# Attention chain in halves of heads, weight products in column halves, and new orders in a recurrent memory attention with its gradients

## The chip, the cores and the metric

The kernel runs on one core of one Trainium2 chip. The metric is the device time of one execution in microseconds (us); a kernel's time is the median of its runs. The core has five engines that work side by side: TensorE (PE in the profile, with its weight loads as PEld), VectorE (DVE), ScalarE (ACT), GpSimd (POOL) and SyncE (SP), which here only issues transfers (DMA). TensorE writes to PSUM, eight banks of 2 KB in each of 128 partitions. VectorE and ScalarE take results out of PSUM.

## The reference

The inputs are x (2048 tokens of 512), a memory of 8 rows, the weights of an attention with 32 heads of 128, those of an MLP with 1792 hidden units, and a gradient of the output. The attention goes over 64 segments of 32 tokens, one after the other, because the first 8 output rows of one segment are the memory of the next:

```python
for s in range(n_seg):                       # 64 segments of 32 tokens
    h = concatenate([mem, xn[:, 32 * s:32 * (s + 1)]])      # 8 + 32 rows
    q, k, v = (einsum('btd,dhe->bhte', h, W) for W in (Wq, Wk, Wv))
    p = softmax(where(mask, q @ k.T * Dh ** -0.5, -1e9))    # 40 x 40 a head
    o = einsum('bhte,hed->btd', p @ v, Wo)
    mem = o[:, :8]; outs.append(o[:, 8:])
out = x + concatenate(outs) + (relu(xn @ w1 + b1) ** 2 @ w2 + b2)   # xn = layernorm(x)
```

The outputs are out and its gradients with respect to x, the first memory, Wq, Wk, Wv, Wo, w1, b1, w2 and b2 for the given output gradient. The backward pass is again a recurrence, over the segments in reverse: the gradient that reaches a segment's memory rows is part of the output gradient of the segment before.

## The kernel before, in words

Five stages follow each other: layernorm and MLP (lines 640 to 910); the forward chain of 64 segments (stage built from line 920, `chain` at L1085); the turning of weights by TensorE transposes (`turn`, L449; `turn_o`, L464; called at L1231, L1232 and L1537); the backward chain (`chain`, L1454); and the weight gradients and layernorm gradient (from L1563).

**What sets the order.** Every piece of work is handed to a planner (`_Plan`, L74) with a cost for each engine that could do it, the keys that it reads and writes, and a priority (0 for the chain of the recurrence, 1 for the rest). The planner's `run` (L152) walks through time with these costs, gives each piece to an engine and writes the instructions of every engine in that order. The order is then fixed: an engine works through its own list and waits at its head. Two lists of numbers, `_FWD` (L27) and `_BWD`, raise or lower the rank of each kind of piece, and `_FWD_RULE`, `_BWD_RULE` and the two `_BIAS` pairs set its other rules.

**Layout.** A segment has 32 tokens and 32 heads. Heads lie as 4 (index j, a quarter of the partitions) by 8 (index i, along the columns). Most matmuls of the chain use TensorE as four column tiles of 128x32, so four matmuls with different j stand beside each other; the profile writes them `128*32`. Data of the two halves i = 0 to 3 and 4 to 7 have separate keys in several places.

**One forward segment** (`chain`, L1085) takes the rows in `hA` (named PA in the profile; one buffer holds a block of four segments) and does, in order: projections to q and k (`proj`, L493, matmuls at L501, two output halves of 512 columns, each 16 matmuls), evictions, transposes (`to_T`, L509, matmuls in L387), evictions; a mask matmul and the scores (L1101, L1109) into one bank of 128x320; the projection to v; then on DVE the maximum (L967), the subtraction (L968), on ACT the exponential (L971), on DVE a copy of the memory columns (L1114), two transposes (L1116, L1117), the sum (L1119) and reciprocal (L1120). `bd_fill` (L601, instructions at L603) writes the probabilities into block-diagonal tiles BDA and BDB, 4 copies of 32x256 each, on any of three engines. `bd` (L580, matmuls L588) multiplies them with v in two halves, DVE scales each half (L593) and transposes it (`sq_T`, L480, instruction L484) into OT. The output projection `wo_part` (L980, matmuls L988) runs 64 matmuls of 256 columns into one bank; ACT or DVE copies the bank to RFA (128x256); 16 small matmuls (L1138) select the memory rows, and one DVE copy (L1142) puts them into `hA` of the next segment. PSUM is dealt as four banks "c" for the chain in a ring, two "f" and two "m" for other work.

**Beside the forward chain** run the attention of the memory rows of whole blocks (`l_qkv`, L1025; `l_attn`, L1041), the block outputs (L1158) and the MLP's weight products (`dw_unit`, L1178, matmuls L1193), which accumulate 448 matmuls of 512 columns in two "m" banks from inputs `sx` loaded by SP.

**One backward segment** (`chain`, L1454) projects the output gradient, forms the gradients of the probabilities, goes back through the softmax, forms the three gradients dN of v, q and k (t = 2, 1, 0; `part_bd`, L1476), transposes each to dT, and sums their products with the weights into one bank "r" (`dh_part`, L1300, matmuls L1307, 64 of 512 columns for each t). Two copies of 256 columns bring the sum to R_A, 32 small matmuls (L1506) select the memory rows, and one DVE copy (L1510) puts them into `gT` for the next segment. SP issues loads and stores, among them the stores of dN (S_GN). Beside it run `l_pre` (L1318) and `l_post` (L1354).

## Time and profile before

| | us |
|---|---|
| runs before the change (3) | 2888.3, 2895.45, 2908.77 |
| median | 2895.45 |
| span of the profiled execution | 2892.0 |
| MLP stage | 0 to 226 |
| forward chain | 228 to 1230 |
| weight turns | 1230 to 1292 |
| backward chain | 1292 to 2306 |
| weight products | 2306 to 2892 |

The profile describes one execution; its own time is the span, 2892.0 us, measured from the first to the last instruction. The page gives the busy time of each engine. A group row has the line, the engine, the operation, what it writes and reads, the shape and the count, then total busy us and mean ns of one, then the idle time of the engine just before and what ended it. A row of the timeline has the start, the length, and what it merges (x16 is sixteen instructions); in square brackets stands the engine's wait before it and the instruction that ended that wait. A row of stages has the stretch, its length, the busy time of PE, PEld, DVE, ACT and POOL with their counts, the granted TensorE clock, the share of the transfer engines and GB/s.

### The profile page before, as it was taken

To read this page: it belongs to the slowest core of one execution; us is meant where nothing else is said; L and a number is where in the kernel's file an instruction comes from. 1 tells how busy PE (TensorE), PEld (TensorE's weight loads), DVE (VectorE), ACT (ScalarE), POOL (GpSimd) and SP (SyncE) were. 2 spreads that over 40 slices of the span, in tenths; PEclk is the share of its full clock that TensorE was granted. 3 is DMA by queue.
4 is the path that set the end of the run, shared out by engine and by line. 5 is a ranking of instruction groups with operands and counts; after the bars stand their busy time and mean duration, and the time that the engine had idled before them with its cause. 6 is when DMAs were issued, how large, how long until landed. Compare 5 with 4: busy or idle time off the path is not lost.

```text
span 2892.0 us, 110768 instructions
## 1 busy us (share of the span) xinstructions
PE 2679.4 (93%) x47273; PEld 1569.0 (54%) x47384; DVE 1366.9 (47%) x3432; ACT 1182.2 (41%) x2442; POOL 779.8 (27%) x1876
## 2 busy tenths in 40 slices
PE   8999999999889999888999989989999899999999
PEld 6665555555555555565555555555555544444444
DVE  5544555554554555574545545445454502232322
ACT  4334444454444554445555555555555510000000
POOL 1102221221221221234444434344343401111111
PEclk9999999999999999999999999999999999999999
DMA  6658777777666676457888888898887799788861
GB/s 205 210 158 238 206 199 200 186 202 189 188 179 181 186 200 181 128 139 215 217 234 219 229 217 227 218 236 233 229 220 227 216 344 301 229 253 264 251 185 44
DMA packets 557573, 606.04 MB, mean 210 GB/s; under 512 B 229926, under 2 KB 358455, under 8 KB 555031
## 3 DMA queue, kind: packets, MB, share of 16 engines
q1 hardware_dynamic: 541654, 544.09, 67.3%
q0 software_dynamic: 15424, 54.87, 5.7%
q8 instruction: 371, 6.08, 0.9%
q14 instruction: 124, 1.01, 0.1%
HBM read 290.14 MB, written 272.12 MB: 194 GB/s over the span
## 4 chain that ended last, share of the span: by engine, by line
PE 61%; DVE 14%; DMA 11%; issue 5%; ACT 4%; POOL 2%; SPq 2%; DVEq 0%; ACTq 0%; POOLq 0%
PE ps L501 13%; PE ps L1671 13%; PE ps L1307 8%; DMA S_GN<-dN 4%; PE ps L588 4%; PE ps L988 4%; PE ps L387 4%; PE ps L1674 4%; PE ps_h L764 3%; PE ps_B L792 2%; PE ps_gxb L792 2%; SPq L447 1%; DMA WA<-S_GN 1%; DMA xs<-S_GON 1%; POOL bVT L1445 1%
## 5 line engine op out<-in xcount | busy, mean ns | idle before, releaser
L501 PE MATMUL ps<-WA,PA 128*32 128x512 bf16 x6144 | 362.5, 380 | 9.0 <-DVE PA L1142 6.5
L1671 PE MATMUL ps<-WA,WB 128*128 128x512 bf16 x1536 | 332.3, 379 | 0.6 <-DVE gwo L391 0.6
L501 PEld LDWEIGHTS <-PA 128*32 128x32 bf16 x8192 | 198.0, 96 | 219.5 <-DVE PA L1510 25.5
L1671 PEld LDWEIGHTS <-WB 128*128 128x128 bf16 x1896 | 185.5, 98 | 225.1 <-issue 1.6
L1307 PE MATMUL ps<-WA,dT 128*32 128x512 bf16 x4096 | 236.1, 380 | 20.7 <-DVE dT L484 18.3
L393 ACT CAST gwo<-ps 128x512 bf16<-128x512 f32 x64 | 33.1, 599 | 515.1 <-PE ps L1671 357.9
L391 DVE CAST gwo<-ps 128x512 bf16<-128x512 f32 x64 | 40.0, 684 | 398.5 <-PE ps L1671 268.3
L393 ACT CAST dN<-ps 128x512 bf16<-128x512 f32 x383 | 200.4, 585 | 48.8 <-DMA S_GN<-dN 43.6
L603 POOL COPY BDL<-dSL 32x64 bf16<-32x64 bf16 x256 | 58.8, 230 | 504.1 <-PE ps L588 485.5
L603 POOL COPY BDA<-PB 32x256 bf16<-32x256 bf16 x127 | 53.9, 424 | 505.4 <-DVE PLp L1114 263.7
L1307 PEld LDWEIGHTS <-dT 128*32 128x32 bf16 x4096 | 103.2, 97 | 131.8 <-DVE dT L484 36.8
L988 PE MATMUL ps<-WB,OT 128*32 128x256 bf16 x4096 | 136.1, 282 | 19.1 <-DVE OT L484 9.2
L1682 POOL DMA_DIRECT2D out_dram<-gwo x96 | 71.3, 751 | 292.8 <-ACT gwo L393 264.1
L1307 PE MATMUL ps<-WA,gOT 128*32 128x512 bf16 x2048 | 139.4, 381 | 8.8 <-DVE gOT L484 6.9
L484 DVE STREAM_TRANSPOSE dT<-dN 128x256 f32<-128x256 f32 x256 | 113.0, 444 | 69.5 <-ACT dN L393 64.4
L501 PE MATMUL ps<-WB,PA 128*32 128x512 bf16 x2048 | 124.0, 380 | 14.1 <-DVE PA L1510 12.3
L988 PEld LDWEIGHTS <-OT 128*32 128x32 bf16 x4096 | 106.8, 100 | 49.8 <-DVE OT L484 31.2
L391 DVE COPY qT<-ps 128x512 bf16<-128x512 bf16 x120 | 50.8, 424 | 163.2 <-PE ps L387 160.2
L393 ACT CAST kN<-ps 128x512 bf16<-128x512 f32 x127 | 74.8, 589 | 107.5 <-PE ps L501 104.7
L393 ACT CAST gON<-ps 128x512 bf16<-128x512 f32 x128 | 74.7, 585 | 107.2 <-PE ps L501 106.8
L484 DVE STREAM_TRANSPOSE gOT<-dN 128x256 f32<-128x256 f32 x128 | 56.3, 440 | 122.4 <-PE ps L1468 79.0
L1193 PE MATMUL ps<-sx,anT 128*128 128x512 bf16 x373 | 107.5, 381 | 4.2 <-DMA sx<-in_grad_out_dram 0.9
(317 smaller groups left out, 5369.4 us busy)
## 6 DMA issues: line engine op xcount, KB each, us to landing
S_GN<-dN SPq DMA_DIRECT2D x192, 256.0 KB
WA<-S_GN SPq DMA_DIRECT2D x160, 256.0 KB
S_K<-kN SPq DMA_DIRECT2D x64, 256.0 KB
S_Q<-qN SPq DMA_DIRECT2D x64, 256.0 KB
S_V<-vN SPq DMA_DIRECT2D x64, 256.0 KB
S_ON<-oN SPq DMA_DIRECT2D x64, 256.0 KB
bqN<-S_Q SPq DMA_DIRECT2D x64, 256.0 KB
bkN<-S_K SPq DMA_DIRECT2D x64, 256.0 KB
```

The source lines that it names most:

```text
L387: nc.tensor.transpose(ps_ap, in_ap, ident[base:base + k, base:base + k])
L393: nc.scalar.copy(out, in_)
L484: self.plan.add({"DVE": 0.36}, lambda e, x=x: nc.vector.transpose(dst[:, x, :, :].rearrange("p i c r -> p (i c r)").bitcast(F32).rearrange ...
L501: nc.tensor.matmul(bk()[32 * j:32 * (j + 1), :], lhsT=win(dc), rhs=Wt(dc, c0), start=(dc == 0), stop=(dc == DC - 1), tile_position=(0, 32 ...
L588: nc.tensor.matmul(bv()[:, n * P:(n + 1) * P], lhsT=B_[:, i, :, :].rearrange("p j k -> p (j k)"), rhs=X[:, i, :], start=(y == 0 and n == 0 ...
L603: self.plan.add(cost or {"ACT": 0.4, "DVE": 0.27, "POOL": 0.42}, lambda e, j=j: {"ACT": nc.scalar.copy, "DVE": nc.vector.tensor_copy, "POO ...
L792: nc.tensor.matmul(bk()[:], lhsT=src[z][:, fc, rc * P:(rc + 1) * P], rhs=Wt[:, fc, :], start=(fc == 0 and first), stop=(fc == FC - 1))
L988: nc.tensor.matmul(bk()[32 * t:32 * (t + 1), :], lhsT=tq(OTt, i, j), rhs=Wo[:, JQ * hs(i) + j, h * HB:(h + 1) * HB], start=(i == 0 and j < ...
L1193: nc.tensor.matmul(bks[x]()[:], lhsT=anT[x][:, c, :], rhs=sx[z][:], start=(c == 0), stop=(c == TC - 1))
L1307: nc.tensor.matmul(bk()[32 * j:32 * (j + 1), :], lhsT=tq(XT, i, j), rhs=wtf(t, i, j), start=(first and i == 0), stop=(last and i == NI - 1 ...
L1671: nc.tensor.matmul(bks[n]()[:], lhsT=HNc[:, rc, dc * P:(dc + 1) * P], rhs=half_of(gns[y], hf), start=(y == 0), stop=(y == NRC - 1))
L1674: nc.tensor.matmul(bks[n]()[:], lhsT=gns[y][:, k * P:(k + 1) * P], rhs=GOc[:, rc, :], start=(y == 0), stop=(y == NRC - 1))
```

## The change

- The forward chain is written as a loop over two halves of heads g. Each half has its own projections, transposes, scores, maximum, subtraction, exponential, copies, transposes, sum, reciprocal, fills (16 of 32x128 in place of 8 of 32x256 for both tiles), products and scaling, in banks fixed by name. q's, k's and v's projections are cut by the pairs (dq, dq+2) of the 128-row input chunks, so that a first piece needs only one half of the new memory rows.
- The output projection of the chain (`wo_half`) is cut into two column halves x of 128, each in its own bank, evicted, selected and copied to `hA` by itself: 128 matmuls of 128 columns in place of 64 of 256.
- "c" has 5 banks and "m" one. `dw_unit` works through column halves y of 256 in that one bank: 896 matmuls of 256 columns in place of 448 of 512, with input rows of 512 B in place of 1 KB in as many transfers.
- In the backward chain, the sum "r" gets two banks and "c" four: `dh_half` makes 128 matmuls of 256 columns for each t in place of 64 of 512, alternating between the banks, and the copies to R_A, the selections and the copies to `gT` are made for each half; the next projection's pieces need one half each.
- Off-chain products of both chains are handed to the planner in finer pieces (`dh_part` and `wo_part` in 8 instead of 4, the gradient of the block probabilities in 4 instead of 1, `diag_own` in 4 instead of 1, block scores in 3 instead of 1; off-chain projections in 4 pieces a half instead of 2).
- The turns of Wk and Wq use one bank instead of two.
- The lists `_FWD` and `_BWD` (200 numbers each) and the rules are other numbers; the order of every engine in both chains follows from them. In the typical forward segment of the changed kernel DVE goes through both maxima, both subtractions, then transposes, copies and fills of the halves, both sums and reciprocals, both scalings, both output transposes; PE's order at the end is x0 with the first heads, x1 with the first heads, a filler, x0 and x1 with the second heads, selection of the first column half, a filler, selection of the second, the next projection. In a backward segment it is both column halves with the first heads, both with the second, the first selection, 8 projection matmuls, the second selection, the other projection matmuls.
- The products with BDA and BDB, and Wo and its gradient, go through the heads in their natural order (`hs`, L625, is no longer used there). The last stage does the same work with its banks in another order.

Instructions of the whole kernel, before and after: TensorE matmuls 45873 and 56817, VectorE 3322 and 4010, ScalarE 2412 and 2687, GpSimd 1881 and 2132, SP 2868 and 2868.

```diff
-_FWD_RULE = (0.563, 0, 2.684, 14.947)
-_FWD_BIAS = (-0.246, -0.25)
+_FWD_RULE = (0.214, 161.741, 17.148, 80.928)
+_FWD_BIAS = (0.058, -0.205)
...
-_BWD_RULE = (0.137, 15.477, 0.734, 9.349)
-_BWD_BIAS = (0.248, 0.016)
+_BWD_RULE = (0, 116.512, 23.186, 141.712)
+_BWD_BIAS = (-0.165, -0.189)
...
+        def proj(self, kind, nm, win, wkeys, Wt, col0, dst, prio, halves=(0, 1), skip=1):
+            for half in halves:
+                bk = self.bank(kind, [P, 512], F32, "ps_" + nm) if isinstance(kind, str) else self.fixed(kind, [P, 512], F32)
+                for dq in range(2 if prio == 0 else 4):
...
+                        for dc in ((2 * dq, 2 * dq + 1) if skip == 1 else (dq, dq + 2)) if prio == 0 else (dq,):
...
+        def bd_half(self, at, g, terms, rk, dst, prio, norm):
+            bv = self.fixed(at, [P, 512], F32)
+
+            def mm(e):
+                for y, (B_, X) in enumerate(terms):
+                    for n in range(JQ):
+                        i = JQ * g + n
+                        nc.tensor.matmul(bv()[:, n * P:(n + 1) * P], lhsT=B_[:, i, :, :].rearrange("p j k -> p (j k)"),
+                                         rhs=X[:, i, :], start=(y == 0 and n == 0), stop=(y == len(terms) - 1),
+                                         skip_group_check=True)
+            self.plan.add(pe(0.45, "f", 0.13), mm, rk, [bv.key], prio)
+            self.plan.add({"DVE": 0.69}, lambda e: nc.vector.tensor_tensor(
+                out=dst[1][:, 4 * g:4 * g + 4, :], in0=bv()[:].rearrange("p (i e) -> p i e", i=JQ),
+                in1=norm[:, 4 * g:4 * g + 4].unsqueeze(2).to_broadcast([P, JQ, P]), op=ALU.mult),
+                [bv.key, ("mxA", g)], [(dst[0], g)], prio, EVLAT)
...
+        def bd_fill_half(self, nm, t, src, g, R):
+            x = slice(JQ * g, JQ * (g + 1))
+            for j in range(JQ):
+                self.plan.add({"ACT": 0.31, "DVE": 0.2, "POOL": 0.31}, lambda e, j=j: {
+                    "ACT": nc.scalar.copy, "DVE": nc.vector.tensor_copy, "POOL": nc.gpsimd.tensor_copy}[e](
+                    q_(t, j)[:, x, j, :], q_(src, j)[:, x]), R, [(nm, j, g)], 0, 0.07)
...
-        sg = Stage(plan, {"c": (0, 4), "f": (4, 2), "m": (6, 2)}, pc.tile([P, 8, 512], F32, name="ps"), 0.9)
+        sg = Stage(plan, {"c": (0, 5), "f": (5, 2), "m": (7, 1)}, pc.tile([P, 8, 512], F32, name="ps"), 0.9)
...
+        def wo_half(x, OTt, ok):
+            bk = sg.fixed(("c", 3 + x), [P, P], F32)
+            for q in range(2):
+                def mm(e, q=q):
+                    for i in range(4 * q, 4 * q + 4):
+                        for j in range(JQ):
+                            for h in range(2):
+                                t = 2 * h + j % 2
+                                c0 = h * HB + x * P
+                                nc.tensor.matmul(
+                                    bk()[32 * t:32 * (t + 1), :], lhsT=tq(OTt, i, j), rhs=Wo[:, JQ * i + j, c0:c0 + P],
+                                    start=(i == 0 and j < 2), stop=(i == NI - 1 and j > 1),
+                                    tile_position=(0, 32 * t),
+                                )
+                A(pe(0.44, "w", 0.13), mm, [(ok, q), "WB"], [bk.key], 0, 0.26)
+            A({"ACT": 0.2, "DVE": 0.2}, lambda e: ev({"DVE": "v", "ACT": "s"}[e], RFA[:, x * P:(x + 1) * P], bk()[:]),
+              [bk.key], [("RFA", x)], 0, 0.07)
...
+            hk = lambda dq: [("hA", p), ("hm", p, v, dq)]
+            for g in range(2):
+                x = slice(JQ * g, JQ * (g + 1))
+                sg.proj(("c", 2 * g), "q", win, lambda dq: hk(dq) + [("WA", 0)] + DLW.get(s, []), wf(0), 0, ("qN", qN), 0, (g,), 2)
+                sg.proj(("c", 2 * g + 1), "k", win, lambda dq: hk(dq) + [("WA", 1)], wf(1), 0, ("kN", kN), 0, (g,), 2)
...
+                bs_ = sg.fixed(("c", (4, 2)[g]), [P, JQ, KA], F32)
+
+                def sc(e, x=x, bs_=bs_):
+                    for j in range(JQ):
+                        nc.tensor.matmul(q_(bs_(), j).rearrange("p i k -> p (i k)"), lhsT=ident[:, 32 * j:32 * (j + 1)],
+                                         rhs=maskA[:, x].rearrange("p i k -> p (i k)"), start=True, stop=False,
+                                         tile_position=(0, 32 * j), skip_group_check=True)
+                    for n in range(JQ):
+                        i = x.start + n
                         for j in range(JQ):
+                            nc.tensor.matmul(q_(bs_(), j)[:, n, :], lhsT=qT[:, i, j, :], rhs=KT[p][:, v, i * JQ + j, :],
                                              start=False, stop=True, tile_position=(0, 32 * j), skip_group_check=True)
+                A(pe(0.14, "w", 0.12), sc, [("qT", g), ("KTA", p, v, g), ("KTL", p, g)], [bs_.key, ("tk", s, g)] + ([("tk", s)] if g else []), 0)
+                sg.proj(("c", g), "v", win, lambda dq: hk(dq) + [("WA", 2)], wf(2), 0, ("vN", vN), 0, (g,), 2)
+                mx, sm, st = sm_t["A"]
+                bc = lambda t, x=x: t[:, x].unsqueeze(2).to_broadcast([P, JQ, KA])
+                A({"DVE": 0.36}, lambda e, x=x, bs_=bs_: V.tensor_reduce(mx[:, x], bs_()[:], axis=AX.X, op=ALU.max), [bs_.key], [("mxA", g)], 0)
+                A({"DVE": 0.36}, lambda e, x=x, bs_=bs_, bc=bc: V.tensor_tensor(out=st[:, x], in0=bs_()[:], in1=bc(mx), op=ALU.subtract),
+                  [bs_.key, ("mxA", g)], [("stA", g)], 0)
+                A({"ACT": 0.33}, lambda e, x=x: nc.scalar.activation(P40[:, x], st[:, x], ACT.Exp, scale=scale),
+                  [("stA", g)], [("P40", g)], 0)
+                A({"DVE": 0.14}, lambda e, x=x: V.tensor_copy(PLp[v][:, x, M * v:M * (v + 1)], P40[:, x, 0:M]),
+                  [("P40", g)], [("PLp", v, g)], 0, 0.07)
+                A({"DVE": 0.24}, lambda e, x=x: V.transpose(PTA[:, x], P40[:, x, M:KA]), [("P40", g)], [("PTA", g)], 0)
+                A({"DVE": 0.24}, lambda e, x=x: V.transpose(PTL[:, x].rearrange("p i k -> p (i k)"), PLp[v][:, x].rearrange("p i e -> p (i e)")),
+                  [("PLp", v, g)], [("PTL", g)], 0)
+                A({"DVE": 0.36}, lambda e, x=x: V.tensor_reduce(sm[:, x], P40[:, x], axis=AX.X, op=ALU.add), [("P40", g)], [("smA", g)], 0)
+                A({"DVE": 0.24}, lambda e, x=x: V.reciprocal(mx[:, x], sm[:, x]), [("smA", g)], [("mxA", g)], 0)
+                sg.bd_fill_half("BDA", BDA, PTA, g, [("PTA", g)])
+                sg.bd_fill_half("BDB", BDB, PTL, g, [("PTL", g)])
+                sg.bd_half(("c", g), g, ((BDB, vLN[p]), (BDA, vN)),
+                           [(n_, j, g) for n_ in ("BDA", "BDB") for j in range(JQ)] + [("vN", g)] + [("vLN%d" % p, h) for h in range(2)],
+                           ("oN", oN), 0, mx)
...
+            for x in range(2):
+                wo_half(x, OT, "OT")
...
+            for y in range(2):
+                bk = sg.fixed(("m", 0), [P, 2, HB], F32)
+                for c in range(0, TC, 2):
+                    z = c // 2 % 5
+                    sg.dma(lambda z=z: sx[z][:].rearrange("p (k d) -> p k d", k=2),
+                           lambda c=c, y=y: src[c * P:(c + 2) * P, y * HB:(y + 1) * HB].rearrange("(k p) d -> p k d", k=2),
+                           [("tk", 0)], [("sx", z)], lat=3.0)
+
+                    def mm(e, k, c=c, z=z, bk=bk):
+                            for x in range(2):
+                                nc.tensor.matmul(bk()[:, x, :], lhsT=anT[x][:, c + k, :], rhs=sx[z][:, k * HB:(k + 1) * HB],
+                                                 start=(c + k == 0 and x == 0), stop=(c + k == TC - 1), skip_group_check=True)
+                    for k in range(2):
+                        A(pe(0.217, "f", 0.11), lambda e, k=k, mm=mm: mm(e, k), [("sx", z), ("anT", 0, c // HC), ("anT", 1, c // HC)], [bk.key], 1, _MMLAT)
...
-        sg = Stage(plan, {"c": (0, 5), "r": (5, 1), "f": (6, 2)}, pc.tile([P, 8, 512], F32, name="ps"), 1.8)
+        sg = Stage(plan, {"c": (0, 4), "r": (4, 2), "f": (6, 2)}, pc.tile([P, 8, 512], F32, name="ps"), 1.8)
...
+        def dh_half(bks, XT, xk, t, first, last):
+            for hf in range(2):
+                for q in range(2):
+                    def mm(e, q=q, hf=hf):
+                        for i in range(4 * q, 4 * q + 4):
+                            for j in range(JQ):
+                                nc.tensor.matmul(bks[hf]()[32 * j:32 * (j + 1), :], lhsT=tq(XT, i, j),
+                                                 rhs=wtf(t, i, j)[:, 2 * hf:2 * hf + 2], start=(first and i == 0),
+                                                 stop=(last and i == NI - 1), tile_position=(0, 32 * j))
+                    A(pe(0.435, "w", _DRAIN), mm, [(xk, q)] + [((t, "WT"), g) for g in range(8 * q, 8 * q + 8)],
+                      [bks[hf].key], 0, _MMLAT)
...
-            bk = sg.bank("f" if sg.rings else "c", [P, NI, KA], F32, "ps_dP")
+            bk = sg.fixed(("c", 2), [P, NI, KA], F32)
...
-            bR = sg.bank("r", [P, D], F32, "ps_dRA")
+            bR = [sg.fixed(("r", hf), [P, HB], F32) for hf in range(2)]
...
-                dh_part("r", "A", dT[t], TK[t], t, first, last, 0, bR)
+                dh_half(bR, dT[t], TK[t], t, first, last)
...
+                    {"DVE": "v", "ACT": "s"}[e], R_A[:, HB * hf:HB * (hf + 1)], bR[hf]()[:]),
+                  [bR[hf].key], [("R_A", hf)], 0, 0.08)
+                    bm = sg.fixed(("c", 2 + hf), [P, 2, M], F32)
+
+                    def gm(e, hf=hf, bm=bm):
+                        for dc in range(2):
                             for g in range(JQ):
+                                c0 = HB * hf + dc * P + 32 * g
+                                nc.tensor.matmul(bm()[32 * g:32 * (g + 1), dc, :], lhsT=R_A[:, c0:c0 + 32], rhs=sel8[:],
+                                                 start=(dc == 0), stop=(dc == 1), tile_position=(0, 32 * g), skip_group_check=True)
+                    A({"DVE": 0.19}, lambda e, hf=hf, bm=bm: V.tensor_copy(
+                        gT[p1][:, 2 * hf:2 * hf + 2, RA * v1:RA * v1 + M], bm()[:]),
+                      [bm.key, ("gT", p1)], [("gm", p1, v1, hf)], 0)
...
-        sg.rings = {"t": [("c", 4), ("f", 1)], "f": [("f", 0)], "c": [("c", x) for x in range(4)]}
+        sg.rings = {"t": [("f", 1)], "f": [("f", 0)], "c": [("c", x) for x in range(4)]}
```

204 lines of the change are left out of this document (81 added, 123 removed), and 51 rows, old and new, of tables (_BWD, _FWD).

## The prediction

> **What bounds the kernel now.** I read the page first, then the busy time by stage, then the chain of the two recurrences in order of time, and last the single groups of instructions by shape.
>
> ```profile
> span 2892.0 us, 110768 instructions
> PE 2679.4 (93%) x47273; PEld 1569.0 (54%) x47384; DVE 1366.9 (47%) x3432; ACT 1182.2 (41%) x2442; POOL 779.8 (27%) x1876
> PE 61%; DVE 14%; DMA 11%; issue 5%; ACT 4%; POOL 2%; SPq 2%; DVEq 0%; ACTq 0%; POOLq 0%
> ```
>
> ```profile
> 0.00:226.00 226.00, 210.60 (x1513) 143.92 (x1537) 123.51 (x479) 84.61 (x209) 36.25 (x85) 0.99 0.61 191
> 228.00:1230.00 1002.00, 914.98 (x20502) 558.91 (x20576) 541.03 (x1326) 484.37 (x962) 212.92 (x439) 0.99 0.69 190
> 1230.00:1292.00 62.00, 53.60 (x1026) 42.44 (x1026) 45.27 (x83) 28.53 (x47) 19.61 (x41) 0.94 0.55 138
> 1292.00:2306.00 1014.00, 924.87 (x21299) 561.02 (x21300) 500.29 (x1280) 544.50 (x1148) 412.05 (x1160) 1.00 0.82 223
> 2306.00:2892.00 586.00, 573.36 (x2942) 261.96 (x2952) 156.84 (x265) 39.54 (x77) 99.00 (x151) 0.99 0.75 234
> ```
>
> The stages are the MLP, the 64 forward segments, the turning of weights, the 64 backward segments and the weight products. The change leaves the matmuls of the first and last alone. A PE that is 91% busy looks like the bound of the two long ones, but a matmul's recorded time holds its latency, so I follow one forward segment instead:
>
> ```profile
> 488.58 0.28 PE L1109 MATMUL ps<-KT,qT 128*32 128x40 bf16 x16
> 489.02 0.49 DVE L967 TENSOR_REDUCE mxA<-ps 128x8 f32<-128x320 f32 x1 [0.49 <-PE ps L1109]
> 489.54 0.49 DVE L968 TENSOR_TENSOR stA<-ps,mxA 128x320 f32<-128x320 f32 x1
> 490.62 0.45 DVE L1116 STREAM_TRANSPOSE PB<-P 128x256 bf16<-128x256 bf16 x1 [0.58 <-ACT P L971]
> 490.99 0.14 DVE L1114 COPY PLp<-P 128x64 bf16<-128x64 bf16 x1
> 491.64 0.55 DVE L603 COPY BDB<-PB 32x256 bf16<-32x256 bf16 x2
> 492.62 0.20 DVE L1120 RECIPROCAL mxA<-smA 128x8 f32<-128x8 f32 x1
> 494.38 0.65 DVE L593 TENSOR_TENSOR oN<-ps,mxA 128x512 bf16<-128x512 f32 x1
> 494.63 0.78 PEld L988 LDWEIGHTS <-OT 128*32 128x32 bf16 x32
> 495.07 0.45 DVE L484 STREAM_TRANSPOSE OT<-oN 128x256 f32<-128x256 f32 x1
> 497.28 0.29 PE L988 MATMUL ps<-WB,OT 128*32 128x256 bf16 x3 [0.67 <-issue]
> 497.66 0.37 ACT L393 COPY RFA<-ps 128x256 f32<-128x256 f32 x1 [2.27 <-PE ps L988]
> 498.62 0.19 DVE L1142 CAST PA<-ps 128x32 bf16<-128x32 f32 x1 [1.73 <-PE ps L1138]
> 498.87 1.48 PE L501 MATMUL ps<-WA,PA 128*32 128x512 bf16 x24
> ```
>
> The last copy (L1142) hands the memory rows to the next segment's projections. Its group:
>
> ```profile
> L1142 DVE CAST PA<-ps x63: 191/192/193, 252.7 to 1212.4; 128x32 bf16<-128x32 f32 x63
> ```
>
> 62 periods in 959.7 us make 15.48 us each. So the stage's length is 63 times a latency loop (projection, scores, softmax, attention, output projection, copy), and other PE work fills its gaps. A shorter loop shortens the stage as long as the filling still fits.
>
> **Forward, softmax stretch.** The softmax instructions are halved and doubled in number. A half is priced by the straight line through two shapes of one operation:
>
> ```profile
> L968 DVE TENSOR_TENSOR stA<-ps,mxA 128x320 f32<-128x320 f32 x64 | 31.5, 491 | 2.2
> L968 DVE TENSOR_TENSOR sumR<-ps,mxL 128x512 f32<-128x512 f32 x16 | 11.0, 688 | 1.3
> L1071 DVE STREAM_TRANSPOSE PTLL<-PLL 128x512 bf16<-128x512 bf16 x16 | 11.4, 711 | 0.5
> L1116 DVE STREAM_TRANSPOSE PB<-P 128x256 bf16<-128x256 bf16 x64 | 28.5, 445 | 34.7 <-ACT P L971 34.7
> ```
>
> (688-491)/192 is 1.03 ns a column, so 160 columns take 327 ns, 163 of them fixed. The transpose gives 312 ns for 128 columns, 179 fixed. In the stretch before, DVE works from 489.02 to 495.52, or 6.50 us, with two waits inside (0.58 for the exponential, about 0.5 ahead of the multiplication). After, the first maximum runs beside the second half's scores, and DVE then goes through the second maximum, two subtractions and two sums (5 x 0.327), four transposes (4 x 0.312), two copies (0.28), some three fills (0.2 each, between half of 0.275 and 0.275), two reciprocals (0.40), two multiplications (1.33) and two output transposes (0.90): 6.39 us with hardly a wait. What halving gains in overlap it pays back in fixed cost. I take 0; bounds are -0.4 (halves that start back to back) and +1.5 us (a half that costs as much as a whole: 5 x 0.16 + 4 x 0.13 + 0.2).
>
> The Trainium skill, "VectorE: DVE Perf Modes", section "The TRN2 errata", warns against just this: each instruction pays its access latency anew, so it advises tiles of 512 elements or more. Its formula gives 58 cycles at 0.96 GHz from SBUF and 120 from PSUM, an estimated 60 ns for a transpose and 125 for a subtraction, less than the 179 and 163 of the rows; by the page the stretch would be an estimated 0.7 us shorter and the whole 44 us faster than my sum. The rows decide.
>
> **Forward, output projection and hand-over.** Before, from the end of the last output transpose (495.52) to the next projection (498.87) pass 3.35 us, 0.67 of it a gap at issue that I leave out as this segment's own: 2.68. After, 128 matmuls of 128 columns stand for 64 of 256. 32 weight loads with 256-column matmuls took 0.78 us, 24.4 ns each; at half the columns 12.2 ns if columns set it, 24.4 if the instruction does. The 16 score matmuls of 40 columns took 0.28 us, and one of them lasts 0.181 by its group:
>
> ```profile
> L1109 PE MATMUL ps<-KT,qT 128*32 128x40 bf16 x2048 | 34.6, 181 | 1.3 <-DVE qT L391 1.2
> ```
>
> So they start under 7 ns apart, and I take 12.2. Then each quarter lasts 0.39 us. Counted from the last output transpose's end, the first heads' quarters end by +0.4 (their transpose ended 0.45 earlier), the second heads' first column half at +0.8 and second at +1.2, with one filler of 0.2 to 0.4 between: +1.0 and +1.5. The first eviction (0.27 for 128 columns instead of 0.37), selection and copy run beside the second column half; the second selection stands ahead of the projection on PE and ends at 1.5+0.1+0.27+0.15, about +2.05. 2.68 less 2.05 is 0.63; I take 0.65 us with bounds 0.3 (more filler) and 1.2 (max and scores gain too). Next would be late the second copy, 0.4 us, hidden by 32 projection matmuls that need only the first memory half (24 of them take 1.48 us in the row above). 63 x 0.65 = **-41 us**, bounds -75 and, with the +1.5 of the stretch, +55.
>
> **Backward.** The end of a light segment:
>
> ```profile
> 2037.15 3.64 PE L1307 MATMUL ps<-WA,dT 128*32 128x512 bf16 x64
> 2040.84 0.65 ACT L393 COPY R_A<-ps 128x256 f32<-128x256 f32 x2 [2.79 <-PE ps L1307]
> 2041.48 0.40 PE L1506 MATMUL ps<-sel,R_A 128*32 128x8 f32 x31
> 2041.97 0.19 DVE L1510 CAST PA<-ps 128x32 bf16<-128x32 f32 x1 [3.44 <-PE ps L1506]
> 2042.22 1.05 PE L501 MATMUL ps<-WB,PA 128*32 128x512 bf16 x16
> ```
>
> From the first of these 64 matmuls to the next projection pass 5.07 us. The time 3.64 less 0.2 of latency is 54 ns a matmul. After, 128 of 256 columns in four runs of 0.86 us alternate between two banks: the first column half is complete at 2.6+0.2, its eviction (0.33) ends at 3.15; the selection stands behind the last run on PE (3.45) and ends at 3.65, the copy at 3.9, the projection starts at about 4.0. The second half's eviction (3.65 to 4.0), selection and copy are over at 4.9, while the 8 projection matmuls of the first half cover 0.43: of the gain of 1.05 up to 0.5 returns as that wait. I take 0.75 us; bounds 0.3 and 1.05. 63 x 0.75 = **-47 us**, bounds -66 and -19, and 0 if transfers set the pace.
>
> Every fourth segment is heavier; there the store of a gradient tile gates the eviction of the next:
>
> ```profile
> ACT dN L393 <- DMA S_GN<-dN: 43.6, 31, 3.0
> ```
>
> In the new order of SP one load stands ahead of the second of these stores in those segments instead of three, some 1 us of issue in 16 segments. Bounds -16 and 0: **-8 us**. The off-chain products in 8, 4, 4 and 3 pieces issue the same matmuls; they cost nothing while PE has something else at hand, and at most a 0.1 us switch of shape each.
>
> **Weight turns.** Those of Wk and Wq get one bank instead of two:
>
> ```profile
> L387 PE MATMUL ps<-ident,WA x337: 216/219/314, 1229.8 to 1279.1; 128*128 128x128 bf16 x169
> L391 DVE COPY WA<-ps x33: 628/691/692, 1230.5 to 1279.4; 128x1024 bf16<-128x1024 bf16 x33
> L393 ACT COPY WA<-ps x10: 1012/1012/1013, 1230.1 to 1273.4; 128x1024 bf16<-128x1024 bf16 x10
> ```
>
> 43 turns in 49.6 us are 1.15 each, with transposes beside evictions. With one bank, 8 transposes (0.45), the copy (0.69 on DVE, 1.01 on ACT) and a hop of 0.1 follow each other: 1.24 to 1.56. On 32 turns +3 to +13: **+8 us**.
>
> **Weight products beside the forward chain.** 896 matmuls of 256 columns for 448 of 512: the same columns and about 2 ns more for each pair, +1. Their inputs come in rows of 512 B instead of 1 KB in as many transfers; the forward stage's transfer share is 0.69, so I price it at 0, with +20 if those transfers are late.
>
> **Sum.** -41-47-8+8+1 = -87 on a span of 2892.0: 2805. The span lies 3.5 under the median of the runs, 2895.45, so 2808.5, about 2808.
>
> **The rivals.** First, *more overlap than I count*: each bound on the good side (-75, -66, -16) with the turns' +8 gives -149, 2746. For it speaks that every stretch of the loop is now in halves; against it that DVE has no gap left in which to do so. If back-to-back instructions hid 0.4 us of fixed cost a segment (the good bound of the stretch) and nothing else changed, it would be 2783, inside my own range. Chance 0.14.
>
> Second, *the gain is there on the chain and something else sets the pace*: the backward stage moves 223 GB/s at a share of 0.82 and a segment cannot be shorter than its transfers. With 0 for the backward stage, its stores included, 2892-41+9+3.5 = 2863; with half of the forward gain 2884; between them some 2875. It shows as waits on DMA. Chance 0.14.
>
> Third, *slower: DVE becomes the forward loop's bound*. Its halves cost nearly what wholes cost (+1.5 us), and off-chain evictions (0.65 us each), which sat in its waits, now delay the chain: +2.2 us in place of 0. 63 x 2.2 = 139 on 2808 gives 2947. It decides from +1.8 us a segment ((87+28)/63). For it: some 45% more DVE instructions in the stage (1326 and about 600, by the order of the two kernels); against it: the straight lines. Chance 0.24.
>
> Fourth, *a floor under each matmul*. At 24.4 ns for 128 columns the output projection keeps twice its time, +1.56 us in 64 segments, 100 us: 2908. The scores at under 7 ns speak against it. Chance 0.04. The Trainium skill, "TensorE: Matmul & The Clock Gate", section "Wait — 56ns, not 53.3ns?", has start-to-start never under some 25 ns; here four column tiles side by side fall below it, so the trace does not agree for tiled matmuls.
>
> **How the numbers follow.** My forecast gets 0.44, with a range of its own of 2765 to 2855. A measurement of this kernel can tell about 1% (29 us) from no change. Faster by more: 0.44+0.14 = 0.58. Within it: the second and fourth, 0.18. Slower: 0.24. The range leaves out the lower part of the first rival (0.07) and the upper half of the third (0.13): 2740 to 2930.
>
> **What would show it.** Forward: L1142's successors come about 14.8 us apart, the wait before the next projection is filled, and DVE's softmax stretch stays near 6.4 us. Backward: about 4.0 us from the first of the last products to the next projection. The turns take some 8 us more. I am wrong if half-size DVE instructions cost over 0.4 us, if off-chain DVE work stands between them, or if PE idles for the second half at each hand-over.

## The result, and the profile after

The changed kernel takes 3054.9 us (median of 4 runs) against 2902.1 of the kernel before in the same rounds: 1.054 times as long, 95% interval 1.050 to 1.058. The prediction was 2808, range 2740 to 2930. The forecast had the wrong sign.

The page of the changed kernel, its first rows and the row of one transfer queue:

```profile
span 3052.9 us, 134268 instructions
PE 2718.3 (89%) x58292; PEld 1810.4 (59%) x58328; DVE 1470.2 (48%) x4120; ACT 1231.9 (40%) x2717; POOL 829.5 (27%) x2127
...
q8 instruction: 457, 7.49, 1.1%
```

The same queue's row on the page of the kernel before:

```profile
q8 instruction: 371, 6.08, 0.9%
```

The last row is one that the prediction didn't read. Queue q8 brings TensorE's instructions: 7.49 MB in 457 transfers are 16 KB each, and 58292 matmuls and 58328 weight loads over 457 are 255 a transfer. I call such a transfer a block.

The stages of the changed kernel (busy time of PE, PEld, DVE, ACT, POOL, clock, transfer share, GB/s); the bounds are moved to its own stages:

```profile
0.00:226.00 226.00, 211.00 (x1511) 144.23 (x1535) 123.57 (x479) 84.67 (x209) 36.38 (x85) 1.00 0.60 190
228.00:1247.00 1019.00, 923.57 (x24933) 605.92 (x24935) 540.65 (x1754) 577.36 (x1338) 261.98 (x701) 0.99 0.66 184
1247.00:1325.00 78.00, 60.66 (x1216) 48.69 (x1205) 53.70 (x110) 33.97 (x64) 31.24 (x62) 0.89 0.56 147
1325.00:2460.00 1135.00, 946.59 (x27568) 746.09 (x27569) 594.85 (x1511) 493.19 (x1023) 401.38 (x1130) 0.98 0.74 200
2460.00:3052.00 592.00, 574.53 (x3077) 264.56 (x3082) 157.23 (x266) 42.12 (x82) 98.53 (x149) 0.99 0.74 233
```

Both chains issue about 49 TensorE instructions a microsecond (49868 in 1019 us, 55137 in 1135), where the kernel before issued 41 and 42. The transfer share of the backward stage fell, so it is not the transfers' volume that holds it up. The waits of TensorE's matmuls in that stage, before and then after (us in total, times, longest):

```profile
PE ps L1307 <- DVE dT L484: 18.1, 14, 2.2
PE ps L501 <- DVE PA L1510: 12.3, 32, 0.5
PE ps L588 <- POOL BDK L603: 9.5, 14, 1.1
```

```profile
PE ps L1376 <- issue: 43.2, 31, 3.0
PE ps L1591 <- issue: 20.3, 15, 2.9
PE ps L1376 <- DVE dT L491: 16.9, 25, 2.3
PE ps L508 <- issue: 16.0, 13, 2.8
```

"issue" means that the profile shows nothing that PE waited for. Summed over all rows of that view, it is 5 us (7 times) in the forward and 6 us (9 times) in the backward stage before, and 52 (53 times) and 112 (90 times) after: 153 us more, where the whole kernel is 161 us longer in these two executions. By stage, the waits grew by 47 us in the forward and 106 us in the backward one, and 62 periods of the chains by 30 and 106 us (table below). One such wait, in the middle of the last products of a backward segment:

```profile
1620.88 2.59 PE L1376 MATMUL ps<-WA,dT 128*32 128x256 bf16 x88
1624.53 1.28 PE L1376 MATMUL ps<-WA,dT 128*32 128x256 bf16 x40 [1.06 <-issue]
1625.62 0.29 PE L1591 MATMUL ps<-sel,R_A 128*32 128x8 f32 x16
```

The 88 and the 40 are one run of 128, 64 for each of the segment's last two gradients. The planner hands them over in pieces of 16, and the break falls inside such a piece, whose inputs are ready as a whole, so no semaphore stands there. A block's transfer on q8 lasted from 1622.34 to 1623.26, and PE went on 1.27 us later. In the backward stage 117 of 183 us in which PE neither loaded nor multiplied (gaps over 0.15 us) end 0.9 to 1.7 us after a block has come; before the change 11 of 78.

### The profile page after: what moved, and what is told of

It is laid out like the page before. It is cut to its first block, busy times and chain, and to the rows that moved or that the text cites. A ratio compares the mean times of both kernels' runs of the same rounds, so it can differ in the third digit from the quotient of the medians.

```text
span 3052.9 us, 134268 instructions
## 1 busy us (share of the span) xinstructions
PE 2718.3 (89%) x58292; PEld 1810.4 (59%) x58328; DVE 1470.2 (48%) x4120; ACT 1231.9 (40%) x2717; POOL 829.5 (27%) x2127
## 2 busy tenths in 40 slices
DMA packets 586342, 607.55 MB, mean 199 GB/s; under 512 B 229925, under 2 KB 387126, under 8 KB 583702
## 3 DMA queue, kind: packets, MB, share of 16 engines
q8 instruction: 457, 7.49, 1.1%
## 5 line engine op out<-in xcount | busy, mean ns | idle before, releaser
L1376 PE MATMUL ps<-WA,dT 128*32 128x256 bf16 x8192 | 255.0, 277 | 52.7 <-issue 34.9
L1376 PEld LDWEIGHTS <-dT 128*32 128x32 bf16 x8192 | 212.2, 98 | 78.2 <-issue 42.2
L630 POOL COPY BDA<-PB 32x128 bf16<-32x128 bf16 x222 | 64.6, 291 | 476.0 <-DVE PLp L1172 241.5
L1053 PE MATMUL ps<-WB,OT 128*32 128x128 bf16 x8192 | 136.8, 220 | 22.5 <-issue 15.4
L1376 PE MATMUL ps<-WA,gOT 128*32 128x256 bf16 x4096 | 134.7, 275 | 15.0 <-issue 8.3
L400 ACT COPY R_A<-ps 128x256 f32<-128x256 f32 x128 | 47.7, 373 | 248.1 <-PE ps L1376 248.1
L1259 PE MATMUL ps<-sx,anT 128*128 128x256 bf16 x896 | 127.9, 274 | 6.4 <-DMA sx<-S_XN 6.0
L1389 PE MATMUL ps<-WA,LT 128*32 128x512 bf16 x1536 | 112.7, 390 | 23.4 <-ACT dLN L400 11.4
L398 DVE COPY KT<-ps 128x512 bf16<-128x512 bf16 x74 | 31.3, 424 | 209.9 <-PE ps L394 197.9
L1376 PEld LDWEIGHTS <-gOT 128*32 128x32 bf16 x4096 | 110.4, 97 | 34.1 <-DVE gOT L491 14.4
```

What stands on the lines that cost most here:

```text
L398: nc.vector.tensor_copy(out, in_)
L400: nc.scalar.copy(out, in_)
L630: self.plan.add({"ACT": 0.31, "DVE": 0.2, "POOL": 0.31}, lambda e, j=j: {"ACT": nc.scalar.copy, "DVE": nc.vector.tensor_copy, "POOL": nc.g ...
L1053: nc.tensor.matmul(bk()[32 * t:32 * (t + 1), :], lhsT=tq(OTt, i, j), rhs=Wo[:, JQ * i + j, c0:c0 + P], start=(i == 0 and j < 2), stop=(i = ...
L1259: nc.tensor.matmul(bk()[:, x, :], lhsT=anT[x][:, c + k, :], rhs=sx[z][:, k * HB:(k + 1) * HB], start=(c + k == 0 and x == 0), stop=(c + k ...
L1376: nc.tensor.matmul(bks[hf]()[32 * j:32 * (j + 1), :], lhsT=tq(XT, i, j), rhs=wtf(t, i, j)[:, 2 * hf:2 * hf + 2], start=(first and i == 0), ...
```

## The experiments

Two theories at first. *Supply*: TensorE's instructions come in blocks of 256, a block takes some microseconds from its request on, and where PE uses up 256 instructions faster than that it stands still. *Waits*: the halves bring new waits, or the shorter VectorE instructions lengthen the chain (the prediction's third rival). The whole table, each row one profiled execution; 62 periods from the copy of the memory rows to that of the next segment, "between" from the last forward to the first backward copy, blocks in these periods (to within one) and PE's matmul waits "issue" in the stages (blank where they weren't summed). With two copies to a segment the second counts. Each ratio is to the runs of before in the same rounds, whose medians lay between 2890 and 2902.

```
                 forward  blocks issue | between | backward blocks issue | median, ratio to before [95%]
before             959.8   156     5.0 |   80.3  |  1009.6   167     6.1 |
after              990.0   191    52.0 |   98.6  |  1115.7   214   112.1 | 3054.9  1.054 [1.050, 1.058]
e1 before dh 256   956.1   156         |   83.5  |  1089.1   213    72.0 | 2974.0  1.028 [1.023, 1.034]
e2 before wo 128   999.4   186    41.4 |   79.7  |  1012.8   167         | 2940.3  1.017 [1.013, 1.022]
e3 after dh 512    984.9   191         |   99.1  |  1031.8   168    20.2 | 2959.5  1.023 [1.018, 1.029]
e4 after wo 256    926.6   160     2.2 |   97.4  |  1105.6   214         | 2983.4  1.033 [1.027, 1.039]
e6 both            931.9   161         |  100.1  |  1042.7   168         | 2915.8  1.007 [1.005, 1.010]
e7 fwd after       981.1   191    43.5 |   84.8  |  1018.3   167         | 2931.9  1.012 [1.008, 1.016]
e8 one wo bank     987.6   162         |   79.8  |  1010.1   166         | 2930.3  1.012 [1.007, 1.016]
e9 four quarters  1083.7   164         |  106.4  |  1022.7   166         | 3059.5  1.058 [1.054, 1.062]
e10 two turn banks 979.2   191         |   85.6  |  1114.5   214         | 3026.1  1.047 [1.044, 1.050]
e11 as e9, later  1155.0   165         |  123.9  |  1012.4   166         | 3147.0  1.088 [1.085, 1.090]
e12 quarters bf16  947.9   157     1.2 |   87.1  |  1012.1   167         | 2899.0  1.000 [0.998, 1.002]
```

The forward chain of the changed kernel stands as it is in four rows (after, e3, e7, e10) and takes 979 to 990 us there, so a single execution of a stage is good to some 10 us.

### Instructions alone, added to the kernel before (e1, e2)

```diff
 e1, dh_part, prio 0                         e2, wo_part "A"
-  matmul(bk[.., 0:512], rhs=wtf(t, i, j))   -  matmul(bk[.., 0:256], rhs=Wo[.., h * HB:(h + 1) * HB])
+  for u in range(2):                        +  for u in range(2):
+    matmul(bk[.., 256 * u:256 * (u + 1)],   +    matmul(bk[.., 128 * u:128 * (u + 1)],
+           rhs=wtf(t, i, j)[:, 2 * u:2 * u + 2])  rhs=Wo[.., h * HB + 128 * u:h * HB + 128 * (u + 1)])
```

> The kernel before, with each 512-column product of the backward chain (line 1307 with dT and gOT) issued as two of 256 columns into the same bank; columns, order of the other engines, waits and result are as before. 6144 matmuls and 6144 weight loads more, 12288 instructions, 48 blocks of 256. Supply theory (PE's instructions come from memory in transfers of 16 KB, 256 instructions each, and PE stands still when the next block is late): the backward stage goes from 167 blocks to 215, as many as the changed kernel has (216), so it gains most of that kernel's 106 us: +70 to +110 us, about 2985. Rival, the hand-over in halves and its waits: nothing of it is here, so within 10 us of 2900. Rival, a fixed cost of each matmul in the array: 6144 times (2 to 3 ns) is 12 to 18 us, more only if the rows show 256-column matmuls over 27 ns apart.

> The kernel before, with each 256-column product of the forward chain's output projection (line 988 with OT) issued as two of 128 columns into the same bank; all else as before. 8192 instructions more, 32 blocks: 161 become 193 in the forward stage, as many as in the changed kernel (195). Supply theory: +20 to +45 us, in the forward stage alone. Rival, waits of the halves: within 10 us of 2900. Rival, a floor of 25 ns under each matmul: +1.5 us a segment, +95 us.

The same columns, banks and waits, in smaller pieces: +84 us (2974.0 against 2890.3) and +50 us, most of it in the stage concerned (80 and 40 us of its 62 periods). A fixed cost of a matmul in the array doesn't explain it: in unbroken runs four matmuls with different j start every 110 ns in e1 against 217 ns for twice the columns before, and every 56 ns in e2 against 111, so a piece costs by its columns once it runs. What is new is the wait before it, 72 us of "issue" in e1's backward stage against 6, part of it in this group:

```profile
L1309 PE MATMUL ps<-WA,dT 128*32 128x256 bf16 x7936 | 240.6, 275 | 31.3 <-DVE dT L484 15.0 <-issue 13.5
```

The second theory's waits are absent here, and 134 us of loss are present, where the change cost 153. e2's loss was 5 us above the expected range.

### Instructions alone, taken from the changed kernel (e3, e4, e6)

```diff
 e3, dh_half                                 e4, wo_half
-  for i in range(4 * q, 4 * q + 4):         -  for i in range(4 * q, 4 * q + 4):
-    matmul(bks[hf] [.., 0:256], half rhs)   -    matmul(bk[.., 0:128], rhs=Wo[.., c0:c0 + P])
+  for i in range(4 * q, 4 * q + 4, 2):      +  for i in range(4 * q, 4 * q + 4, 2):
+    matmul(bw[.., 0:512], whole rhs)        +    matmul(bw[.., 0:256], rhs=Wo[.., h * HB:(h + 1) * HB])
```

> The changed kernel, with the backward chain's products for half of the heads only, but 512 columns wide: columns and time in the array, order, waits, banks and evictions are those of the changed kernel, its 12288 instructions fewer. It leaves out the other heads' share of the products. Supply theory: 216 blocks become 168 as before the change, the stalls go, -80 to -115 us, about 2955. Rival, waits of the halves or the DVE chain: they are all still there, within 10 us of 3055.

> The changed kernel, with the forward chain's output projection for half of the heads only, but 256 columns wide: columns, order, waits and evictions are those of the changed kernel, 8192 instructions fewer. It leaves out the other heads' share. Supply theory: 195 blocks become 163, -30 to -50 us in the forward stage alone. Rival, waits of the halves or the DVE chain: within 10 us of 3055.

> The changed kernel with both edits of the two experiments before: half of the heads, twice the columns, in the output projection and in the backward products (the other heads' shares are left out). Instructions in both chains about as before the change, all halves and hand-overs as after. Supply theory, added up from the two: 3055-95-72 = 2888, so 2870 to 2900. If the hand-over in halves gains what was predicted once supply is out of the way: 2808 and the 10 us that the turns cost more, about 2820. If the halves' waits cost by themselves: over 2920.

All halves, banks, waits and the order stay, half of the instructions of one product go: -95 us (2959.5) and -72 us (2983.4) against 3054.9. The 3054.9 is from other rounds; by the ratios to the kernel before it is about 88 and 61 us, and the stage concerned got 84 and 63 us shorter. e4 gave more than the expected 30 to 50. e4's forward stage has lost its "issue" (2.2 us) and is 33 us shorter than that of the kernel *before* the change; PE's waits there are now small ones on fills and copies:

```profile
PE ps L618 <- POOL BDB L630: 14.8, 39, 1.7
PE ps L618 <- ACT BDB L630: 3.4, 9, 0.7
PE ps L394 <- DVE lN L398: 3.3, 2, 1.7
```

So the halves do shorten the forward loop; what they cost there is instructions. In the backward stage they don't shorten it: with the blocks of before (168) e3's 62 periods still take 22 us more. There the longest waits of PE's matmuls are for transfers and what hangs on them, and ACT waits for a store:

```profile
PE ps L1490 <- DMA xs<-S_GON: 21.3, 14, 3.3
PE ps L1390 <- ACT dLN L400: 19.5, 11, 3.1
```

```profile
ACT dLN L400 <- DMA S_GNL<-dLN: 67.1, 13, 7.0
```

The same waits for xs and for the store of dLN in the kernel before:

```profile
PE ps L1406 <- DMA xs<-S_GON: 3.7, 3, 1.4
ACT dLN L393 <- DMA S_GNL<-dLN: 9.7, 14, 1.3
```

e6 came out at 2915.8, above its 2870 to 2900 and far from the 2820 that the full gain of the halves would have given. Against the kernel before, its forward periods are 28 us shorter, its backward periods 33 us longer and the stage between 20 us longer. So the added instructions are about 139 us of the changed kernel's time (3054.9 to 2915.8), and the rest of what is missing from the forecast isn't theirs.

### The supply by itself (e5)

```diff
+  for m in range(6144):
+      matmul(bank[32 * j:32 * (j + 1), 0:40], lhsT=[128 x 32], rhs=[128 x 40])    # j = m % 4
+  ...                                  # 64 loads of a weight-gradient input on SP, the first waits for the run above
+  for m in range(6144): the same matmul
```

> The kernel before, with two runs of 6144 matmuls of 40 columns (as the scores' shape) added at its end, 12288 instructions or 48 blocks each; the first while no transfers run, the second beside 64 loads of a whole weight-gradient input each. The cost of the supply by itself. If PE's own pace bounds (under 7 ns for a load and its matmul), each run takes about 41 us. If the supply has a fixed pace, both take the same, 48 times 3.4 us or more, 163 us up. If the supply waits its turn among the other transfers, the first takes at most 163 us (3.4 us a block, the shortest distance in the two profiles) and the second about 240 (5.0 a block, as in the stages with stalls).

The two runs in stretches without and with transfers, and the queues in the first and in the second stretch:

```profile
2910.00:3068.00 158.00, 55.33 (x5632) 50.01 (x5632) 0.00 (x0) 0.00 (x0) 0.00 (x0) 0.50 0.02 5
3080.00:3160.00 80.00, 24.63 (x2524) 22.33 (x2523) 0.00 (x0) 0.00 (x0) 0.00 (x0) 0.50 0.65 197
```

```profile
q8 instruction: 44, 0.72, 1.8%
```

```profile
q1 hardware_dynamic: 8481, 15.44, 62.6%
q8 instruction: 19, 0.31, 2.1%
```

A stretch of the first run, matmuls and then weight loads:

```profile
2928.82 1.26 PE L1702 MATMUL ps<-WB 128*32 128x40 bf16 x128 [2.49 <-issue]
2932.29 1.26 PE L1702 MATMUL ps<-WB 128*32 128x40 bf16 x128 [2.22 <-issue]
```

```profile
2928.81 1.14 PEld L1702 LDWEIGHTS <-WB 128*32 128x32 bf16 x128 [2.61 <-issue]
2932.29 1.14 PEld L1702 LDWEIGHTS <-WB 128*32 128x32 bf16 x128 [2.34 <-issue]
```

PE runs through exactly 256 instructions in about 1.1 us and then stands still for 2.4 us or more, 44 times in a row. A block's transfer starts 0.1 us after the last of the 256 (median of the 44; 0.5 at most), and PE goes on 1.4 us after that transfer's end. So it is the block that PE waits for, and not a steady cost of each instruction. With no data transfers, 44 blocks of 256 took 158 us, 3.6 us a block or 14 ns an instruction; PE was busy for a third of it. (The granted clock was 0.50 in both stretches; in the changed kernel, at 0.98 to 0.99 in its chains, the shortest distance of two blocks is much the same, 3.3 us.) Beside loads at a share of 0.65 it was 80/19 = 4.2 us a block. So when PE does nothing but run through instructions, a block has a pace of its own, and transfers make it slower by a sixth. The second run had transfers for its first half only, so its whole length (184 us for 48 blocks) doesn't test the expected 240. This is one execution.

### Which stage (e7), and versions with a complete result (e8, e9, e11, e12)

e7 puts the forward chain of the changed kernel ahead of the turns and the backward chain of the kernel before. e8 also makes the output projection in one bank of 256 columns, with two evictions. e9, e11 and e12 keep two column halves x in two banks but sum each head quarter j in its own 32 rows:

```diff
-  matmul(bk[32 * t:32 * (t + 1), 0:128], rhs=Wo[.., c0:c0 + P])    # t = 2 * h + j % 2, for h in 0, 1
+  matmul(bk[32 * j:32 * (j + 1), 0:256], rhs=Wo[.., x * HB:(x + 1) * HB])
```

> The forward chain of the changed kernel with the turns of Wk and Wq, the backward chain and the lists of the kernel before. Supply theory: the forward stage keeps its 30 us, the backward stage and the turns go back: 2895+30, 2915 to 2940. If the two stages' losses are not separate, over 2950.

> As the one before, but with the output projection in 64 matmuls of 256 columns into one bank and only its eviction, selection and copy in two column halves: 8192 instructions fewer. Supply theory: the 50 us of the split go from the forward stage and with them the overlap of the two column halves (0.4 us in 63 segments, 25 us): 2880 to 2915. Theory that halved softmax instructions lengthen the chain: at least 2925.

> The forward chain in halves with a complete result and without the added instructions, and the backward chain of the kernel before. The output projection adds up each head quarter in its own 32 rows (64 matmuls of 256 columns a segment, still in two column halves), the selection adds four parts in place of two, the off-chain projection takes 32 matmuls of 512 columns, the stores of partial sums double to 256 KB a segment and GpSimd adds twice as often. 445 TensorE instructions more than before in all, against 22000 in the changed kernel. Supply theory: the forward stage comes to within 15 us of the experiment that had half of the heads (927), so 925 to 945 for 62 periods against 960, and the whole to 2860 to 2885. Theory that the halves themselves cost (halved softmax, waits): 2895 or more.

> As the experiment with four head quarters, but the planner is told that the loads of the partial sums take 10 us to land, so that GpSimd's additions stand later in its queue, behind the block-diagonal fills that waited for them (up to 9.7 us, 103 us in all by the wait of the weight loads for BDB). If that queue was the forward stage's loss: 62 periods in 925 to 960 us in place of 1084, the whole at 2860 to 2900, stalls at blocks under 15 us. If the four quarters or the order cost by themselves: over 2950.

> The forward chain in halves, in the changed kernel's own order, with 7300 TensorE instructions fewer and a complete result, and the backward chain of the kernel before. Each head quarter adds up in its own 32 rows, and the four partial sums are kept in bfloat16, so that stores and loads have the size and number that they had and no buffer is shared; GpSimd makes three additions in place of two. Compared with the same pair of chains at 191 forward blocks (2932): supply theory, the forward stage goes from 981 to within 20 us of 927 and the whole to 2870 to 2895. If it is the order or the partial sums that cost, as in the two versions with four quarters before: 2925 or more.

e7 separates the stages as expected: the forward stage keeps most of its loss, the other two give nearly all of theirs back. e8 missed the range of the supply theory, and its 2930.3 lies in that of the rival (2925 or more, softmax in halves lengthens the chain): with 162 blocks its forward stage is no shorter (987.6). Its mean period is 0.45 us longer than before: the stretch from the first maximum to the last output transpose takes 7.31 us against 6.57, the hand-over from there to the first copy 2.53 against 2.51, the rest 6.09 against 6.40. So what e4 gains at the hand-over is missing here, and the softmax stretch is longer than in e4 (7.01, mean) as well. e9 missed by far: 164 blocks, and 1084 us. Its weight loads wait for fills that stand behind additions on GpSimd, which wait for loads:

```profile
POOL sumR L1221 <- DMA sumR<-S_RO: 175.2, 27, 14.5
...
PEld L615 <- POOL BDB L627: 102.6, 73, 9.7
```

I took that queue for the cause, and that fell too: e11, with the additions later, needs 1155 us. What e8, e9 and e11 have in common is that the planner gave another order of VectorE's instructions than the one its lists were made for; e9 and e11 also share one buffer among the softmax and four rounds of loads and additions. Which of it costs how much was not separated. e12 keeps the changed kernel's order (VectorE's list is nearly the same but for shapes), shares nothing and has 157 blocks: its forward stage takes 947.9 us, 33 less than e7's, with "issue" down from 43.5 to 1.2, and the whole equals the kernel before (1.000). Both are just outside what was expected (within 20 us of 927, 2870 to 2895). Of its 12 us on the forward stage of before, 7 are lost between the chains and 5 to 6 in backward chain and tail. None of the versions beats the kernel before.

### Two banks for the turns (e10)

```diff
-  sg.rings = {"t": [("f", 1)], ...
+  sg.rings = {"t": [("f", 1), ("r", 1)], ...
```

> The changed kernel with two banks in turn for the transposes of Wk and Wq (the second is one of the two banks that the backward sums use later). One-bank theory for the stage between the chains: 48 turns at 1.57 us go back towards 1.19 for the 32 of them, -8 to -18 us, 3037 to 3047; the chains stay as they are. Rival, the stage is bound by the copies on VectorE (0.69 us each): within 4 us of 3055.

The turns of the changed kernel:

```profile
L394 PE MATMUL ps<-ident,WA x384: 216/219/314, 1265.8 to 1340.5; 128*128 128x128 bf16 x192
L398 DVE COPY WA<-ps x41: 628/691/693, 1266.5 to 1340.9; 128x1024 bf16<-128x1024 bf16 x41
L400 ACT COPY WA<-ps x7: 1012/1012/1030, 1269.1 to 1321.3; 128x1024 bf16<-128x1024 bf16 x7
```

48 copies in 75 us, 1.57 each; the kernel before makes its 48 between 1222.9 and 1280.1, 1.19 each. The mean hides a difference: the first 16 copies, those of Wv, weren't slowed (20 us against 27 before). The 32 of Wk and Wq that follow start 1.68 us apart against 0.87 before, and 0.76 in e10. Two banks bring the stage between the chains from 98.6 to 85.6, 13 us, as expected; the 32 turns themselves gain 29, half of it given back before the first backward copy. The whole fell by more than expected, to 3026; the other 11 us of the profiled execution are in the forward stage, which the edit doesn't touch, and within the spread of that stage.

## Why the prediction was wrong

**The step that failed** is the price of the doubled products: the prediction counted their time in the array and put the supply of their instructions at nothing. "The 16 score matmuls of 40 columns ... start under 7 ns apart, and I take 12.2", and in the backward stage "128 of 256 columns in four runs of 0.86 us": both price a matmul by its columns and by the spacing inside a short burst. As a price in the array that about held: 14 ns for 128 columns and 28 for 256 in the unbroken runs of e2 and e1, where the prediction has 12.2 and 27. But a burst of 32 instructions tells nothing of the supply: in e5, too, 256 instructions go through in 1.1 us, and then PE waits for the next block.

An added block cost 1.7 to 2.0 us on average: 84 us for 46 blocks in e1, 50 for 30 in e2, 84 and 63 us of their stages for 46 and 31 in e3 and e4. That is half of the 3.6 us that it costs in e5, where there is no other work beside which a block could come. The change added 35 blocks to the forward and 47 to the backward chain, and taking out 76 of the 82 brought 139 us (e6). One output projection after the change is 128 matmuls and 128 weight loads, a whole block, and lasts 1.8 us in the array; a block takes 3.6 to 4.2 to come. The kernel before used a block in 6.1 us of both chains on average, the changed one in 5.2.

The profiled executions moved by +30, +106 and +18 us in the forward chain, the backward chain and between them, where the sum had -41, -55 and +8. With the supply out of the way (e6) it is -28, +33 and +20. So without the added instructions the change is about even (1.007), and they make it 1.054. Of the 247 us between 2808 and 3054.9 they are 139; the other 108 lie mostly in the backward chain.

The Trainium skill, "Runtime: NRT & Kernel Launch", section "Instruction fetch mechanics", says that engines fetch 16 KiB blocks of 256 instructions while they execute, and that crossing a block's bound is mostly hidden. The size agrees (16.4 KB on q8). Hidden it was in the kernel before, 11 us of "issue"; at 49 instructions a microsecond it was not, 164 us.

**Forward hand-over: right in mechanism.** From the last product to the first copy it took 1.25 us before (median) and 0.42 after, while the products themselves end 1.70 instead of 1.13 after the last output transpose. From that transpose's end to the next projection the prediction had 2.68 and 2.05 us; the medians are 2.81 before, 2.63 after and 2.03 with supply out of the way (e4). There the forward stage gains 33 us, where I had said 41. That the two are near is in part luck: in the mean period of e4 the hand-over to the first copy gains 0.80 us and the stretch from there to the maximum 0.18, and the softmax stretch loses 0.44.

**Softmax stretch: mis-sized.** Said 0, bounds -0.4 and +1.5; measured 7.04 us from the first maximum to the last output transpose against 6.50 (medians), the same in e4 (7.02). This is the third rival's place, at a quarter of its price.

**Backward hand-over: there, and without effect.** The text ahead of the prediction counts 64 matmuls of 512 columns for each gradient. There are 32, and 64 of 256 after the change: the row of 64 that the prediction reads holds the last two gradients. From the first product of the last gradient to the end of the first copy it took 3.28 us before (median), 2.34 after and 2.29 in e3: 0.9 to 1.0 less, where 1.05 was forecast. The second copy ends 1.03 us after the first (0.98 in e3), and from there to the next segment's products of the last gradient it takes 12.27 us before, 12.98 after and 12.53 in e3. The means, which add up to the period, are 3.40 + 12.89 = 16.3 us before, 2.99 + 1.52 + 13.48 = 18.0 after and 2.22 + 1.17 + 13.25 = 16.6 in e3: even at the old number of blocks the segment gives back more than the first copy gained. The -47 assumed that the rest of the segment would stay. In e3 nearly all waits for transfers (xs, S_GNL, S_GN) lie in the heavy one of every four segments, which takes 0.8 us more than before. The other three have hardly any, and they take -0.05, +0.4 and +0.2 us, where 0.75 less was forecast. So late transfers explain at most 13 of the 22 us and nothing of the missing gain in the lighter segments. Whether the new order or the halves take it back was not tested; the cause stays open.

**The stores of dN**: the wait fell from 43.6 to 21.6 us as said; no gain of 8 us can be seen behind the rest. **The turns**: +8 said, and the stage between the chains took 18 more. The 1.15 us that the prediction starts from mixes the turns of Wv with those of Wk and Wq. The latter had 0.87 and came to 1.68, 26 us on 32 turns. **The weight products** beside the chain (+1) were not tried alone.

**The rivals.** None named the cause. The fourth had the right object, instructions and not columns, and was set aside with the burst of score matmuls; at 1.7 to 2.0 us for each of the 82 added blocks it would have been the sum's largest term. The third had the right sign with the wrong mechanism.

## What to carry to other kernels

Before cutting a matmul in pieces, divide the stage's time by its blocks of 256 TensorE instructions (the instruction queue's row gives their number): here 6.1 us a block left 5 to 6 us of such waits in a chain, and 5.2 left 52 and 112. A loop that is bound by latency can be cut finer only as far as the instruction supply goes, and halves that overlap are worth what they save only if the pieces don't add matmuls. A wait that the profile calls "issue" in the middle of a run of like matmuls was the sign of it here.

## What the runs showed of the hardware that was not expected

- Of all the changed kernel's transfers the instruction blocks are 1% in volume (7.49 of 607.55 MB), and the added ones cost about 139 us of its time (e6): a block's transfer lasts about 1 us, but the next one starts 3.3 us or more after the last (e5 and the changed kernel). Where PE has nothing else to wait for, 256 instructions need 3.6 us without and 4.2 us with data transfers at a share of 0.65.
- In such a stretch a block's transfer starts only when the 256 instructions before it have been run through (0.1 us after the last of them, e5).
- PE goes on 1.2 to 1.6 us after the end of the block's transfer: 109 of the changed kernel's 183 us of backward gaps end in that narrow stretch.
